# Gram products made one chunk per chunk, eight chunks ahead instead of ten

## Chip, cores and metric

The kernel runs on one core of a Trainium2 chip. The metric is the device time of one execution in microseconds (us); lower is better. Engines are named as the profile names them: PE (TensorE matmul), DVE (VectorE), ACT (ScalarE), POOL (GpSimd), SP (SyncE, which issues nearly all DMAs).

## What is computed

Three layers stand one behind the other: a delta-rule attention over 32 sequences (4 batches of 8 heads, 768 steps, head dimension 48), a mixer with two 768 x 768 token matrices, and a feed-forward layer with 1536 hidden columns. The change touches the first alone:

```python
k_n = k / (np.linalg.norm(k, axis=-1, keepdims=True) + 1e-06)
for t in range(S):
    y[:, :, t] = np.einsum('bhd,bhde->bhe', q[:, :, t], state)
    v_old = np.einsum('bhde,bhd->bhe', state, kt)
    state = state + bt[:, :, :, None] * np.einsum('bhd,bhe->bhde', kt, vt - v_old)
```

## The kernel before

**Chunks and sets.** The 768 steps are cut into NC = 24 chunks of 32. Inside a chunk the recurrence becomes a triangular system: its 32 x 32 matrix is made of the Gram products of the chunk's keys, and it is inverted once. Four chunks form a set (NS = 6 sets, 0 to 5); set s holds chunks 4s to 4s+3. `inverse_work(s)` inverts all matrices of a set at once on DVE, with part of the products on POOL, and ends in the transposed inverse `pt` (line 425). The chunk of index c needs the `pt` of set c // 4.

**The chunk loop** (lines 604 to 650) runs over c = 1 to 23. A chunk has two half steps, one for each half h of the sequences. In a half step PE computes `RW` from the state (line 437), DVE subtracts it from the values (`Rs`, line 440), PE multiplies by the inverse (line 452), ACT copies the product into `bdw` (line 458), PE adds to the state (`S`, line 466) and ACT copies the state into `bds` (line 471). PE takes the halves in turn: `S` of the half step before, then the product with `pt`, an output product, then `RW` of the next half step. In what follows, (h,c) is the half step h of chunk c, and the DVE rows `Rs`, two to a chunk, mark the time at which it begins.

**Gram products.** `a_work(c)` (line 162) computes for a later chunk the products of its keys with block diagonal tiles `bdk` (line 174): 16 matmuls; ACT copies them out into `G_sb` (keys with keys) and `mt` (keys with queries), and POOL masks `mt`. There are two `bdk` tiles, filled from DRAM by `spread(c + 2)` at the end of `a_work(c)` (line 155, two DMAs on the SP queue). So each tile is filled again only after the Gram products that read it.

**The order of DVE's inversion** is set by a planner. `Stream` (line 51) holds the items of all sets in a list of stages: A and B of a set, then C of that set together with A of the next (C is drawn first), then B of the next. Each item has an estimated cost. In each half step `dv.run(budget)` issues items for 3.08 us (2.3 us from chunk 14 on); what an item costs beyond the budget is kept as a debt in `due`, and the next half step starts with it. Some items are not `ready` before something else has been issued: the first item of A, `tg` (line 260, the transposition of `G_sb` into `Gi`), wants the Gram products of all four chunks of its set issued, that is `4 * s + 3 in done`. Where nothing is ready, `run` stops and the rest of the budget is lost.

**Forced ends.** At the end of a set, `pt` must exist for the next chunk, so the loop issues whatever is left, without a budget, before it goes on:

```python
        if (c % 4 == 3 and s + 1 < NS) or c == 18:
            while s + 1 not in PT:
                if not dv.step():
                    norms()
```

This debt stands in `due` as well. The last set is forced at c = 18, as the pools of the inversion are closed there (`mid.close()`), and the first weights of the mixer are loaded into memory that comes free then (lines 1156 to 1160).

Of the kernel before, what the change touches and what calls it, by code (L numbers as in the profile page):

```python
# [16 lines left out]
NC = 24  # L17
# [75 lines left out]
def attention(ctx, tc, kq, ktok, vin, betai, maskin, x, psa, late=None):  # L93
# [32 lines left out]
    def load_kq(c, part=slice(0, 2)):  # L126
        if c < NC:
            if c not in KQ:
                KQ[c] = ring(c).tile([128, 2, 4, 4, 32], F32, name="kqt")
            nc.sync.dma_start(out=KQ[c][:, part], in_=kq[c][:, part])  # L130

    def load_kt(c):
        if c < NC:
            KT[c] = ktp.tile([128, 4, 2, D], F32, name="ktt")
            nc.sync.dma_start(out=KT[c], in_=ktok[c])

    def load_v(c):
        if c < NC:
            V[c] = vp.tile([128, 8, D], F32, name="vt")
            nc.sync.dma_start(out=V[c], in_=vin[c])  # L140

    def scale_v(c):
        if c < NC:
            k = c % 4
            nc.gpsimd.tensor_tensor(out=V[c], in0=V[c], in1=bc(NT[c // 4][:, 8 * k:8 * k + 8].unsqueeze(2), [128, 8, D]),
                                    op=ALU.mult)
# [3 lines left out]
    def spread(c):  # L150
        if c >= NC:
            return
        for e in range(2):
            ee = slice(64 * e, 64 * e + D)
            nc.sync.dma_start(out=bdk[c % 2][ee, e], in_=kq[c, ee].rearrange("p k g r i -> p k (g r) i"))
# [6 lines left out]
    def a_work(wk, c):  # L162
        hold = {}
        dense = c >= 4

        def first():
            MT[c] = ring(c).tile([128, 4, 2, 32], F32, name="mt")
            hold[0] = psa.tile([128, 4, 2, 64], F32, name="pa", tag="pa")
            if not dense:
                hold[1] = psy.tile([128, 4, 2, 64], F32, name="py")  # L170

        def mm(g):
            for r in range(4):
                nc.tensor.matmul(hold[0][32 * r:32 * r + 32, g, :, :].rearrange("p e (k i) -> p e k i", k=2),  # L174
                                 KQ[c][:, 0, g, r, :], bdk[c % 2][:, :, :, 4 * g + r, :], start=True, stop=True)

        def mm1(g, e):
            for r in range(4):
                nc.tensor.matmul(hold[e][32 * r:32 * r + 32, g, e, 32:64], KQ[c][64 * e:64 * e + D, 0, g, r, :],
                                 KQ[c][64 * e:64 * e + D, 1, g, r, :], start=True, stop=True)  # L180

        def ev(src, e0, ne):
            if ne == 2:
                t = src.rearrange("p g e i -> p (g e) i")
                nc.scalar.copy(out=G_sb[c // 4 % 2][:, 8 * (c % 4):8 * (c % 4) + 8, :], in_=t[:, :, 0:32])
                nc.scalar.copy(out=MT[c].rearrange("p g e i -> p (g e) i"), in_=t[:, :, 32:64])
            else:
                nc.scalar.copy(out=MT[c][:, :, e0, :], in_=src[:, :, e0, 32:64])

        def fin():  # L190
            masks.append(c)
            if step[0] >= 0:
                cut()
            if dense:
                done.add(c)
                spread(c + 2)

        wk.add(0.0, first)
        if dense:
            for g in range(4):  # L200
                wk.add(0.29, lambda g=g: mm(g))
            wk.add(0.0, lambda: ev(hold[0], 0, 2))
        else:
            for g in range(4):
                for e in range(2):
                    wk.add(0.19, lambda g=g, e=e: mm1(g, e))
            for e in range(2):
                wk.add(0.0, lambda e=e: ev(hold[e], e, 1))
        wk.add(0.0, fin)
# [3 lines left out]
    def cut():  # L213
        while masks:
            t = MT[masks.pop(0)].rearrange("p g e i -> p (g e) i")
            nc.gpsimd.tensor_tensor(out=t, in0=t, in1=bc(mask, [128, 8, 32]), op=ALU.mult)
# [226 lines left out]
    def W(h, c, Rs):  # L443
        W_mm(h, c, Rs)
        W_out(h, c)
# [43 lines left out]
    def ym_work(wk, c):  # L489
        def m(e):  # L490
            for g in range(4):
                nc.tensor.matmul(Y[c][32 * g:32 * g + 32, e, :, :], MT[c][:, g, e, :],  # L492
                                 bdw[g // 2][c % NB][:, 2 * (g % 2) + e, :, :], start=(c == 0 and e == 0),
                                 stop=(e == 1),                                 skip_group_check=True)

        def ev():
            ys = p2.tile([128, 2 * 4 * D], F32, name="ys")
            nc.scalar.copy(out=ys, in_=Y[c].rearrange("p e r d -> p (e r d)"))
            o = 32 * (c % 4)
            for g in range(4):  # L500
                nc.sync.dma_start(out=x[c // 4][o:o + 32, g, :], in_=ys[32 * g:32 * g + 32, :])

        for e in range(2):
            wk.add(0.4, lambda e=e: m(e))
        wk.add(0.0, ev)
# [27 lines left out]
    def norms():  # L533
        for s in sorted(norm):
            if ("tg", s) in done:
                norm.pop(s)()
        while pend:
            pend.pop(0)()
# [65 lines left out]
    for c in range(1, NC):  # L604
        s = c // 4
        step[0] = c
        load_kq(c + 11)
        load_v(c + 5)
        scale_v(c + 2)
        load_kt(c + 2)  # L610
        wa, wm, wq = Work(), Work(), Work()
        for n in {1: (9, 10), 2: (11, 12)}.get(c, (c + 10,)):
            if n < NC:
                a_work(wa, n)
        ym_work(wm, c - 1)
        yq_work(wq, c)
        R0 = R(0, c)
        budget = 2.3 if c >= 14 else 3.08
        if c % 4 == 1 and c > 1 and s + 1 < NS:
            while ("tg", s + 1) not in done:  # L620
                dv.step()
        dv.run(budget)
        if late:
            late(c, 0)
        wa.run((0.0 if c == 2 else 0.42) * wa.left())
        S(1, c - 1)
        W(0, c, R0)
        norms()
        wm.flush()
        R1 = R(1, c)  # L630
        dv.run(budget)
        if late:
            late(c, 1)
# [4 lines that stand above are left out]
        wa.flush()  # L638
        S(0, c)
        W(1, c, R1)  # L640
        norms()
        wq.flush()
        if c == 13:
            soon.close()
        if c == 18:
            mid.close()
        if c == 19:
            early.close()
        if late:
            late(c, 2)  # L650
# [474 lines left out]
def build(tc, a):  # L1125
# [8 lines left out]
    with tc.manual_schedule(), outer:  # L1134
# [12 lines left out]
        wts = Weights(nc, None, wide)  # L1147

        def late(c, k):
            if (c, k) == (13, 2):  # L1150
                xp2 = ph1.enter_context(tc.tile_pool(name="x_", bufs=1, **R))
                x.extend(xp2.tile([128, 4, C], F32, name=f"x{t}") for t in (4, 5))
            if (c, k) == (18, 2):
                nc.gpsimd.memset(ones.bitcast(F32), 1.0)
                nc.scalar.copy(out=ones, in_=ones.bitcast(F32))
                wts.st = ph1.enter_context(tc.tile_pool(name="st", bufs=1, **R))
                mx.load_theta(ph1, tc, a["wth"], wts)
                wts.load()
                nc.sync.dma_start(out=ident, in_=a["ident"])
                nc.sync.dma_start(out=g, in_=a["g"])  # L1160
            if (c, k) == (19, 2):
                mx.open(ph1, tc)
                for s in range(3):
                    mx.load_w(s, a["wtok"], mx.cst if s < 2 else None, wts)
                wts.load()
            if c > 19 or (c, k) == (19, 1):
                wts.step()
            if (c, k) == (16, 2):
                nc.scalar.activation(out=warm, in_=warm, func=AF.Sin)
            if (c, k) == (20, 2):  # L1170
                mx.trans(0)
            if (c, k) == (21, 2):
                mx.theta(0)
                mx.angles(0)
                mx.trans(1)
            if (c, k) == (22, 1):
                mx.sines()
            if (c, k) == (22, 2):
                mx.cosines()
            if (c, k) == (22, 2):  # L1180
                mx.turn(0)
                mx.rest(0)
            if (c, k) == (23, 0):
                mx.theta(1)
                mx.angles(1)
            if (c, k) == (23, 1):
                mx.sines()
            if (c, k) == (23, 2):
                mx.cosines()
# [42 lines left out]
        n = len(MIX)  # L1232
# [115 lines left out]
```

## Time and profile before

| | |
|---|---|
| time, median of 3 runs | 786.51 us (785.75 to 788.28) |
| the profiled execution's own time | 786.73 us |
| its span, first to last instruction | 784.8 us |
| busy share of the span: PE, DVE, ACT, POOL | 90%, 66%, 45%, 27% |
| mean granted clock of PE | 0.969 |

The profile is of one execution. Times inside it are counted from the start of its span; its own time is 1.9 us longer than the span. The chunk loop lies at about 43 to 230 us, the mixer follows to about 425 us, then the feed-forward layer. PE's share is a mean over these stages and says nothing of the chunk loop by itself.

### The profile page before, as it was taken

What the parts mean: (1) busy time and instruction counts of PE and PEld (TensorE: products, weight loads), DVE (VectorE), ACT (ScalarE), POOL (GpSimd) and SP (SyncE); (2) the same over time, 40 slices, a digit from 0 to 9 for tenths busy, and PEclk for the clock granted to TensorE, in tenths of its full rate; (3) what the DMA queues carried; (4) which work ended last, traced back from release to release, by engine and by line L of the source; (5) the groups of instructions that cost most, each with busy time, mean ns of one, the idle gap of its engine ahead of it and who ended that gap; (6) DMA issues with size and microseconds to landing.
All of it is one profiled execution on the core that took longest, in us unless ns stands there. A gap on an engine that the chain in (4) does not pass through costs nothing.

```text
span 784.8 us, 18939 instructions
## 1 busy us (share of the span) xinstructions
PE 709.4 (90%) x7955; PEld 655.4 (84%) x7956; DVE 517.8 (66%) x875; ACT 356.9 (45%) x785; POOL 213.2 (27%) x234
## 2 busy tenths in 40 slices
PE   4577887777778999999997999999999999999997
PEld 3455555554468999999997999999999999999997
DVE  7987989986877888888876755435353534444342
ACT  2276776786775766654444433131322222131211
POOL 5854755744020001211111433113131221121120
PEclk8699999999989999999999999999999999999999
DMA  8975767234444223532432220000000000000000
GB/s 250 248 225 172 201 189 214 83 86 137 153 152 162 88 75 101 165 118 80 121 101 81 101 81 5 26 1 31 1 31 1 31 1 30 1 9 24 1 31 30
DMA packets 29716, 71.39 MB, mean 91 GB/s; under 512 B 4928, under 2 KB 17472, under 8 KB 29632
## 3 DMA queue, kind: packets, MB, share of 16 engines
q1 hardware_dynamic: 29632, 70.19, 29.0%
q8 instruction: 62, 1.02, 0.6%
q14 instruction: 22, 0.18, 0.1%
HBM read 56.02 MB, written 9.44 MB: 83 GB/s over the span
## 4 chain that ended last, share of the span: by engine, by line
PE 64%; DVE 15%; DMA 6%; ACT 6%; issue 5%; POOL 2%; SPq 1%; ACTq 0%; DVEq 0%; POOLq 0%
PE ph L1071 19%; PE acc L1090 19%; PE y L957 11%; PE pc L1012 5%; PE pth L897 3%; DMA bdk<-kq 3%; DVE prod L369 2%; ACT bdw L458 2%; DMA raw<-wtok 2%; PE py L492 1%; PE S L466 1%; PE pa L174 1%; DVE t L797 1%; PE RW L452 1%; DVE Ti L378 1%
## 5 line engine op out<-in xcount | busy, mean ns | idle before, releaser
L957 PE MATMUL y<-w,zh 128*128 128x384 f32 x576 | 154.8, 342 | 3.4 <-DVE u L966 2.4
L1090 PE MATMUL acc<-hh,f 128*128 128x384 f32 x576 | 147.0, 336 | 0.0
L1076 DVE SCALAR_TENSOR_TENSOR hl<-ph,hh 128x384 fp32r<-128x384 f32 x96 | 52.4, 553 | 114.5 <-ACT hh L1075 114.5
L1075 ACT ACTIVATE hh<-ph 128x384 fp32r<-128x384 f32 x96 | 46.7, 491 | 163.0 <-PE ph L1071 163.0
L1071 PE MATMUL ph<-xh,f 128*128 128x384 f32 x576 | 116.4, 337 | 0.4 <-DVE u L966 0.4
L957 PEld LDWEIGHTS y<-w,zh 128*128 128x128 f32 x576 | 105.8, 190 | 4.2 <-issue 2.7
L1090 PEld LDWEIGHTS acc<-hh,f 128*128 128x128 f32 x576 | 104.5, 188 | 0.0
L1071 PEld LDWEIGHTS ph<-xh,f 128*128 128x128 f32 x576 | 101.9, 188 | 0.7 <-issue 0.7
L957 PE MATMUL y<-w,zl 128*128 128x384 f32 x288 | 97.7, 339 | 2.4 <-DVE zl L938 2.4
L1090 PE MATMUL acc<-hl,f 128*128 128x384 f32 x288 | 96.9, 336 | 0.0
L1071 PE MATMUL ph<-xl,f 128*128 128x384 f32 x288 | 65.7, 336 | 0.0
L458 ACT COPY bdw<-RW 32x192 f32<-32x192 f32 x192 | 59.5, 310 | 13.6 <-PE RW L452 11.0
L957 PEld LDWEIGHTS y<-w,zl 128*128 128x128 f32 x288 | 54.6, 190 | 3.0 <-DVE zl L938 3.0
L471 ACT COPY bds<-S 48x384 f32<-48x384 f32 x92 | 43.5, 472 | 29.0 <-PE S L466 27.4
L466 PE MATMUL S<-bdw,ktt 128*48 128x192 f32 x368 | 42.0, 351 | 14.4 <-ACT bdw L458 14.3
L1090 PEld LDWEIGHTS acc<-hl,f 128*128 128x128 f32 x288 | 54.0, 188 | 0.0
L806 POOL TENSOR_TENSOR t<-t,g 128x384 f32<-128x384 f32 x12 | 15.3, 1279 | 135.3 <-DVE t L798 123.3
L1071 PEld LDWEIGHTS ph<-xl,f 128*128 128x128 f32 x288 | 51.6, 188 | 0.0
L452 PEld LDWEIGHTS RW<-Rs,pt 32*32 32x32 f32 x1472 | 19.8, 109 | 36.6 <-DVE Rs L440 28.5
L452 PE MATMUL RW<-Rs,pt 32*32 32x48 f32 x1472 | 26.4, 210 | 21.4 <-DVE Rs L440 21.0
L466 PEld LDWEIGHTS S<-bdw,ktt 128*48 128x48 f32 x368 | 20.8, 128 | 28.7 <-ACT bdw L458 22.2
L1100 POOL TENSOR_TENSOR o<-u,o 128x384 f32<-128x384 f32 x21 | 20.8, 1017 | 85.0 <-DVE o L1099 85.0
(165 smaller groups left out, 1305.8 us busy)
## 6 DMA issues: line engine op xcount, KB each, us to landing
kqt<-kq SPq DMA_DIRECT2D x20, 512.0 KB, 5.5
raw<-wtok SPq DMA_DIRECT2D x12, 768.0 KB, 4.7
raw<-wff SPq DMA_DIRECT2D x12, 768.0 KB, 4.9
bdk<-kq SPq DMA_DIRECT2D x40, 192.0 KB, 4.0
vt<-vin SPq DMA_DIRECT2D x24, 192.0 KB, 4.9
ktt<-ktok SPq DMA_DIRECT2D x24, 192.0 KB, 4.6
x<-ys SPq DMA_DIRECT2D x96, 48.0 KB, 2.5
flat<-t SPq DMA_DIRECT2D x12, 384.0 KB, 5.5
```

The source lines that it names most:

```text
L452: nc.tensor.matmul(RW[h][rr, 1, j, :], PT[c // 4][rr, m0 + j, :], Rs[rr, j, :], start=True, stop=True)
L458: nc.scalar.copy(out=b[rr, :, r, :], in_=RW[h][rr, 1, :, :])
L466: nc.tensor.matmul(S_ps[h][64 * e:64 * e + D, g, :], KT[c][:, 2 * h + g, e, :], b[:, 2 * g + e, :, :], start=(c == 0 and g == 0), stop=Tru ...
L471: nc.scalar.copy(out=n[ee, :, e, :], in_=S_ps[h][ee, :, :].rearrange("p g (r d) -> p (g r) d", r=4))
L897: nc.tensor.matmul(ps, l[:, k], self.tw[w][:, k], start=(n == 0), stop=(n == 8))
L957: nc.tensor.matmul(self.Y[q], l[:, ri, 128 * k:128 * k + 128], self.W[s][w][:, 2 * ri + h], start=(first and w == ri == 0 and l is zh), st ...
L1012: nc.tensor.matmul(ps, self.wc[w][:, k, 128 * e:128 * e + 128], r[:, k], start=(n == 0), stop=(n == 8))
L1071: nc.tensor.matmul(ps, w[:, 0, 128 * k:128 * k + 128], r[:, k], start=(n == 0), stop=(n == 8))
L1075: nc.scalar.activation(out=hh, in_=ps, func=AF.Relu)
L1076: nc.vector.scalar_tensor_tensor(out=hl, in0=ps, scalar=0.0, in1=hh.bitcast(F32), op0=ALU.max, op1=ALU.subtract)
L1090: nc.tensor.matmul(self.ACC[j][e], w[:, 1, 128 * e:128 * e + 128], r, start=(f == 0 and n == 0), stop=(f == NF - 1 and n == 2))
L1100: (nc.vector if j == NJ - 1 else nc.gpsimd).tensor_tensor(out=o, in0=u[:, e], in1=o, op=ALU.subtract)
```

## The change

Before, chunk 1 makes the Gram products of chunks 9 and 10, chunk 2 those of 11 and 12, and every later chunk c those of c + 10. Now every chunk c makes those of c + 8. The last one (chunk 23) is thus made in chunk 15 instead of 13, so the pool of the `bdk` tiles (`soon`) is closed at c = 15, and the tiles x4 and x5, which take its memory, are made there too.

```diff
         wa, wm, wq = Work(), Work(), Work()
-        for n in {1: (9, 10), 2: (11, 12)}.get(c, (c + 10,)):
-            if n < NC:
-                a_work(wa, n)
+        if c + 8 < NC:
+            a_work(wa, c + 8)
         ym_work(wm, c - 1)
...
         wq.flush()
-        if c == 13:
+        if c == 15:
             soon.close()
...
         def late(c, k):
-            if (c, k) == (13, 2):
+            if (c, k) == (15, 2):
                 xp2 = ph1.enter_context(tc.tile_pool(name="x_", bufs=1, **R))
```

Since the first item of a set waits for its four Gram products, the planner puts DVE's work in another order. Three places show it, all on DVE. In the rows, `Rs` is the subtraction that starts a half step, `Gi<-G` is `tg`, `XT` and `Ti` are the inversion's products and sums, `s`, `rc`, `nb`, `N` belong to the norms at the start of A, `prod` (DVE) and `prodp` (POOL) are its product tiles.

First, the end of set 1, in chunk 3. Before, between half step (0,3) and (0,4):

```order
L378 TENSOR_REDUCE XT<-prodp 128x16x4
L260 STREAM_TRANSPOSE Gi<-G_133 128x1024
L369 TENSOR_TENSOR prod<-R,XT 128x1024
L369 TENSOR_TENSOR prod<-R,XT 128x768
L440 TENSOR_TENSOR Rs_1223<-vt,RW_127 128x192
L279 TENSOR_SCALAR s_1225<-s_1199 128x32
L378 TENSOR_REDUCE Ti_132<-prod 128x4x16
L283 RECIPROCAL rc<-s_1225 128x32
L378 TENSOR_REDUCE Ti_132<-prod 128x4x16
L284 TENSOR_SCALAR sh<-s_1225 128x32
L425 STREAM_TRANSPOSE pt<-Ti_132 128x32x32
L440 TENSOR_TENSOR Rs_1309<-vt,RW_126 128x192
```

And now, from the same sum of XT on, as far as (1,4):

```order
L378 TENSOR_REDUCE XT<-prodp 128x16x4
L369 TENSOR_TENSOR prod<-R,XT 128x1024
L369 TENSOR_TENSOR prod<-R,XT 128x768
L378 TENSOR_REDUCE Ti_132<-prod 128x4x16
L440 TENSOR_TENSOR Rs_1175<-vt,RW_127 128x192
L378 TENSOR_REDUCE Ti_132<-prod 128x4x16
L425 STREAM_TRANSPOSE pt<-Ti_132 128x32x32
L440 TENSOR_TENSOR Rs_1251<-vt,RW_126 128x192
L260 STREAM_TRANSPOSE Gi<-G_133 128x1024
L440 TENSOR_TENSOR Rs_1314<-vt,RW_127 128x192
```

The transposition of set 2 and its first norms have moved from between the last steps of set 1 to behind its `pt`. The same happens at the ends of sets 2, 3 and 4.

Second, chunk 16. Before, from (0,16) to (0,17), set 5 stands at the end of A and in B:

```order
L440 TENSOR_TENSOR Rs_3143<-vt,RW_126 128x192
L312 TENSOR_TENSOR prod<-N_200,Ti_132 128x196
L313 TENSOR_REDUCE Ti_132<-prod 128x4x7
L369 TENSOR_TENSOR prod<-Gi,Ti_132 128x256 x2
L378 TENSOR_REDUCE XT<-prod 128x2x8x4
L440 TENSOR_TENSOR Rs_3204<-vt,RW_127 128x192
L378 TENSOR_REDUCE XT<-prodp 128x2x8x4
L369 TENSOR_TENSOR prod<-R,XT 128x256 x2
L378 TENSOR_REDUCE Ti_132<-prod 128x2x4x8
L440 TENSOR_TENSOR Rs_3271<-vt,RW_126 128x192
```

Now, from the `pt` of set 4 to the first norm behind (0,17):

```order
L425 STREAM_TRANSPOSE pt<-Ti_131 128x32x32
L440 TENSOR_TENSOR Rs_3105<-vt,RW_126 128x192
L440 TENSOR_TENSOR Rs_3155<-vt,RW_127 128x192
L260 STREAM_TRANSPOSE Gi<-G_134 128x1024
L440 TENSOR_TENSOR Rs_3217<-vt,RW_126 128x192
L279 TENSOR_SCALAR s_3219<-s_3184 128x32
```

Between (0,16) and (1,16) nothing of the inversion stands any more, and set 5 only begins behind (1,16).

Third, the end of set 5 in chunk 18. Before, from (0,18) to (0,19):

```order
L440 TENSOR_TENSOR Rs_3392<-vt,RW_126 128x192
L378 TENSOR_REDUCE XT<-prodp 128x16x4
L369 TENSOR_TENSOR prod<-R,XT 128x1024
L369 TENSOR_TENSOR prod<-R,XT 128x768
L440 TENSOR_TENSOR Rs_3456<-vt,RW_127 128x192
L378 TENSOR_REDUCE Ti_132<-prod 128x4x16 x2
L425 STREAM_TRANSPOSE pt<-Ti_132 128x32x32
L440 TENSOR_TENSOR Rs_3536<-vt,RW_126 128x192
```

Now the last twelve of the sixteen rows from (1,18) to (0,19); `Rs` of (1,18) stands four rows ahead of the first:

```order
L369 TENSOR_TENSOR prod<-R,XT 128x256 x2
L378 TENSOR_REDUCE Ti_132<-prod 128x2x4x8
L378 TENSOR_REDUCE Ti_132<-prodp 128x2x4x8
L369 TENSOR_TENSOR prod<-Gi,Ti_132 128x1024
L369 TENSOR_TENSOR prod<-Gi,Ti_132 128x768
L378 TENSOR_REDUCE XT<-prod 128x16x4 x2
L378 TENSOR_REDUCE XT<-prodp 128x16x4 x2
L369 TENSOR_TENSOR prod<-R,XT 128x1024
L369 TENSOR_TENSOR prod<-R,XT 128x768
L378 TENSOR_REDUCE Ti_132<-prod 128x4x16 x2
L425 STREAM_TRANSPOSE pt<-Ti_132 128x32x32
L440 TENSOR_TENSOR Rs_3536<-vt,RW_126 128x192
```

Before, three rows of the inversion stood in the last half step of chunk 18; now all of B and C of set 5 does, in one piece with no `Rs` inside it. From (0,19) on, DVE's rows are the same as before.

## Rows read from the trace of the kernel before

**Rows 1.** Busy time by stretch: span part, length, engines (count), PE clock, DMA.

```profile
72.20:163.43 91.23, 73.87 (x2216) 51.79 (x2216) 83.09 (x172) 66.09 (x184) 52.76 (x65) 0.94 0.60 170
163.43:185.95 22.52, 16.12 (x488) 10.60 (x488) 19.41 (x28) 18.52 (x48) 13.28 (x16) 1.00 0.31 86
...
425.00:784.00 359.00, 353.63 (x2019) 352.75 (x2019) 162.51 (x277) 97.19 (x186) 71.37 (x67) 1.00 0.08 28
```

**Rows 2.** What DVE waited for from 72.2 to 163.5: total, times, longest.

```profile
DVE Ti L309 <- POOL N L303: 2.1, 4, 0.5
DVE Rs L440 <- PE RW L437: 1.9, 4, 0.5
DVE prod L369 <- ACT R L327: 1.8, 3, 0.7
```

**Rows 3.** Timeline, DVE: start, length, row, [idle before]; (0,2), XT, (0,3), (1,3), (0,4), (0,16), (0,19).

```profile
50.29 0.35 DVE L440 TENSOR_TENSOR Rs<-vt,RW 128x192 f32<-128x192 f32 x1 [1.34 <-PE RW L437]
...
57.67 0.67 DVE L378 TENSOR_REDUCE XT<-prodp 128x64 f32<-128x512 f32 x1
61.74 0.35 DVE L440 TENSOR_TENSOR Rs<-vt,RW 128x192 f32<-128x192 f32 x1 [3.40 <-PE RW L437]
...
67.44 0.35 DVE L440 TENSOR_TENSOR Rs<-vt,RW 128x192 f32<-128x192 f32 x1 [0.70 <-PE RW L437]
...
72.20 0.36 DVE L440 TENSOR_TENSOR Rs<-vt,RW 128x192 f32<-128x192 f32 x1
...
163.43 0.35 DVE L440 TENSOR_TENSOR Rs<-vt,RW 128x192 f32<-128x192 f32 x1 [0.51 <-PE RW L437]
...
185.95 0.31 DVE L440 TENSOR_TENSOR Rs<-vt,RW 128x192 f32<-128x192 f32 x1
```

**Rows 4.** Timeline, PE, in chunks 2 and 3.

```profile
60.95 0.27 PE L481 MATMUL py<-bds,kqt 128*32 128x96 f32 x2 [1.68 <-issue]
...
62.73 0.65 PE L174 MATMUL pa<-bdk,kqt 128*32 128x128 f32 x16 [1.09 <-DMA bdk<-kq]
```

**Rows 5.** Timeline, DVE, the end of set 1 (first row) and of set 5.

```profile
64.27 2.47 DVE L369 TENSOR_TENSOR prod<-R,XT 128x1024 f32<-128x1024 f32 x2
...
177.41 0.41 DVE L378 TENSOR_REDUCE XT<-prodp 128x64 f32<-128x256 f32 x1
177.93 3.19 DVE L369 TENSOR_TENSOR prod<-R,XT 128x1024 f32<-128x1024 f32 x2
...
184.04 2.01 DVE L425 STREAM_TRANSPOSE pt<-Ti 128x1024 f32<-128x1024 f32 x1 [0.66 <-POOL Ti L385]
```

**Rows 6.** Timeline, DVE, transpositions of sets 2 and 5, set 4's last sum and pt.

```profile
62.34 2.01 DVE L260 STREAM_TRANSPOSE Gi<-G 128x1024 f32<-128x1024 f32 x1
...
151.26 1.99 DVE L260 STREAM_TRANSPOSE Gi<-G 128x1024 f32<-128x1024 f32 x1
153.16 0.92 DVE L378 TENSOR_REDUCE Ti<-prod 128x64 f32<-128x768 f32 x1
...
155.08 2.12 DVE L425 STREAM_TRANSPOSE pt<-Ti 128x1024 f32<-128x1024 f32 x1
```

**Rows 7.** Timeline, PE, two half steps of chunks 16 and 17.

```profile
164.06 0.86 PE L466 MATMUL S<-bdw,ktt 128*48 128x192 f32 x8 [0.76 <-ACT bdw L458]
...
167.34 0.86 PE L466 MATMUL S<-bdw,ktt 128*48 128x192 f32 x8 [0.76 <-ACT bdw L458]
```

**Rows 8.** Timeline, DVE, where B of set 5 begins.

```profile
164.48 0.98 DVE L369 TENSOR_TENSOR prod<-Gi,Ti 128x256 f32<-128x256 f32 x2
```

**Rows 9.** Timeline, SP's queue, the mixer's first weights.

```profile
186.08 0.33 SPq L717 DMA_DIRECT2D raw<-wth  x1
```

**Rows 10.** Busy time by stretch: the half step behind pt of sets 1, 2, 3.

```profile
72.20:75.00 2.80, 2.39 (x84) 1.93 (x86) 2.15 (x12) 2.32 (x8) 0.63 (x1) 1.00 0.94 230
103.00:106.30 3.30, 2.85 (x81) 2.24 (x81) 2.99 (x13) 1.71 (x5) 0.89 (x2) 0.73 0.94 270
130.90:134.20 3.30, 2.90 (x92) 2.83 (x96) 2.99 (x13) 1.24 (x4) 0.84 (x2) 0.64 0.46 120
```

## The prediction

> **What bounds the kernel now.** I read the busy time by stretch first. From 425 us on PE is busy 353.63 of 359.00 us, so that part only shifts. In the chunk loop, from half step (0,4) to (0,16), DVE is busy 83.09 of 91.23 us, PE 73.87 and ACT 66.09 [rows 1]. The table of waits says why DVE isn't busy there: 2.1 us for POOL, 1.9 for PE and 1.8 for ACT, 5.8 together [rows 2]. The loop is thus paced by DVE, which has a fixed list of work (the inversions) to do before set 5's pt. The question is how much DVE idles on the way to that pt. As marks I take the starts of three half steps on DVE: (0,4) at 72.20, (0,16) at 163.43 and (0,19), the first row behind set 5's pt, at 185.95 [rows 3]. The DVE rows before (0,2) stand in the same order before and after; behind (0,19) too.
>
> **1. Up to (0,4): the double load goes.** Before (0,3) DVE is done at 58.34 (57.67 + 0.67) and waits 3.40 us for PE, and 0.70 more at (1,3) [rows 3]. PE in turn stands still in chunks 2 and 3: 1.68 us in the output products and 1.09 for a bdk transfer [rows 4]. Chunk 2 issued two sets of Gram products; with one set in chunks 1 and 2 each, no bdk tile is wanted right behind its refill. I let both waits fall to 0, and the 1.34 us at (0,2) by half, 0.7 (ends 0 and 1.34). (0,3) then comes at 57.7.
>
> From there set 1 ends without set 2's rows in between, so the last sum of XT lies 0.6 us behind (0,3), at 58.3. What then ends last is POOL: at the end of set 5, where nothing was woven in before either, pt begins 6.2 us behind the end of that sum (177.41 + 0.41 to 184.04), and it waits 0.66 us for POOL's share [rows 5]. So pt begins at 64.5, and 1.9 us later (184.04 to 185.95) comes (0,4), at 66.4: **5.8 us earlier** than now.
>
> **2. From (0,4) to (0,16).** DVE's work here is now 91.23 - 5.8 = 85.4 us. Added are the transposition of set 2 (1.9 us, 62.34 to 64.27) and three of its norm rows (0.6, an estimate from the time that is left up to (0,4)), which stood before (0,4). Taken out is what set 5 had done by (0,16): from 151.26 to 163.43 are 12.2 us; less two waits of 0.5, three Rs of 0.3, set 4's last sum (0.8) and its pt (2.0) [rows 6], 7.5 remain. That makes 85.4 + 2.5 - 7.5 = 80.4.
>
> One price is new. Where the transposition stood between XT and the two products prod<-R, these took 2.47 us; where they follow XT directly, and so run beside POOL's first product on the same tiles, 3.19 [rows 5]. Sets 2 and 3 change from the one to the other (set 4 ended in the direct order already): 1.4 us. Work is then 81.8.
>
> The waits, for each of the three sets 2, 3, 4: for N on POOL 0.5 (2.1 by four), for R on ACT 0.6 (1.8 by three), for pt on POOL 0.7. For PE it was 0.5 a time. Now there is less to fill the half steps behind pt: the first has only the transposition, 1.9 us and 0.3 for Rs, while a half step that PE and ACT pace takes 3.28 us (164.06 to 167.34, with PE waiting 0.76 for ACT in each) [rows 7]. That could idle 1.1 us in the first and about as much in the next two, yet debts of time from longer half steps close part of it. I take 1.5 us a set, between 0.5 (as now) and 3.0. Chunk 15, with its budget of 2.3 us, gets 1.0 besides (3.28 - 2.3). Together 3 x 3.3 + 1.0 = 10.9, and the stretch is 81.8 + 10.9 = **92.7 us** against 91.2. (0,16) falls at 159.1, still 4.3 us early.
>
> **3. From (0,16) to (0,19): here the lead is missed.** Set 4's forced end leaves a debt, so the first half step of chunk 16 gets no DVE work at all, the second only the transposition, and the two of chunk 17 and the first of 18 some 2 us of small rows each. None fills 3.28 us, so these five half steps go at the pace of PE and ACT: 16.4 us. Then all of B and C of set 5 stands between (1,18) and (0,19). Its work I take from now: of 22.52 us DVE is busy 19.41 [rows 1]; less six Rs of 0.3 and the two rows ahead of B (0.8, as B begins at 164.48) [rows 8], 16.9. With one Rs (0.3) and pt's wait on POOL (0.9, as the Rs that now hides part of it moves away) the piece takes 18.1. The stretch is 34.5 us against 22.5: **12.0 longer**.
>
> **Behind (0,19)** nothing covers it: the mixer's first weights are issued at 186.08, right as set 5's pt (184.04 + 2.01) has ended, since they go into its memory [rows 9]. So what (0,19) loses the end loses. The later closing of the bdk pool costs nothing: x4 is first written in chunk 17, when the last Gram products (chunk 15) are two chunks back. Chunks 14 and 15 get 16 matmuls of Gram products each, two ACT copies and one POOL mask; PE waits 0.76 us per half step there [rows 7], which hides the matmuls, and if the copies aren't hidden, that is within the 1.5 us above.
>
> **Sum:** -5.8 + 1.5 + 12.0 = +7.7 us. The profiled execution took 786.73 us, 0.2 above the median of the runs, so the forecast is 794.4 us.
>
> **Rivals.**
>
> *A colder PE.* Behind pt of sets 2 and 3 PE's granted clock is 0.73 and 0.64 over the next half step, so part of it went at 1.2 GHz; behind set 1's it is 1.00 (2.4 GHz), and 81 matmuls take 2.85 us of PE where 84 took 2.39 [rows 10]. Today DVE's own work covers that. With less to do behind each pt, it shows: some 0.5 us in each of two half steps, behind four ends of sets, 4 us: 798.4. For it speaks that PE will wait longer for each pt; against it that set 1's restart was not cold.
>
> The Trainium skill ("TensorE: Matmul & The Clock Gate", section "What's actually happening") says that a gate passes half the clock's pulses unless the array is kept busy. By that rule every restart here is cold and the time is this rival's 798.4, and not 794.4; the rows agree in two cases of three, which is why it gets a chance of its own, and not the forecast.
>
> *The half step has no floor (the other side).* If 3.28 us is itself only what DVE leaves to PE and ACT, then the half steps shrink to DVE's rows. PE's waits (3 x 1.5 + 1.0) and those for R (1.8) vanish, and the five half steps of part 3 take 1.9 us each, 9.5 in place of 16.4: 14.2 us less than forecast, 780.2, faster than now. It decides from an average of about 2.1 us in those five on, if the waits vanish too. Against it: PE waits for bdw, not for Rs, in a row of half steps of equal length [rows 7].
>
> *The late pt is partly absorbed.* Behind 186 us the mixer's preparation also waits for transfers. If half of the 7.7 us fell into such waits, 790.6; if nearly all, about 787.5. Against it stands that the first of these transfers itself waits for pt [rows 9].
>
> **How the numbers follow.** The forecast, with its own spread of 790 to 799, gets 0.70; the colder PE 0.15 (797 to 802); absorption 0.10 (of it 0.05 within 2.4 us of now); no floor 0.05 (0.04 faster). Under 0.3% (2.4 us) a measurement of this kernel can hardly tell from no change. That gives faster 0.04, same 0.06, slower 0.90. The unknown costs give as bounds: at the low end PE's waits of part 2 at 0.5 a set (-3.0), the wait at (0,2) gone (-0.7) and the half steps of part 3 at 3.0 (-1.4), 789.3; at the high end 3.0 a set (+4.5) and the full wait at (0,2) (+0.7), 799.6. The range is 789.5 to 799.5; it leaves out no floor, most of the absorption and the upper part of the colder PE.
>
> **What would show it.** Right, if (0,4) comes near 66.4, (0,16) near 159 and (0,19) near 194 us, if the wait of 3.40 us at (0,3) is gone, if DVE does nothing of the inversion between (0,16) and (1,16), if sixteen rows in one piece of some 18 us end at set 5's pt with PE waiting, and if the mixer's first weights are issued right behind it. Part 1 is wrong if PE still stands still in chunk 2; part 2, if waits for PE between (0,4) and (0,16) sum to under 2 or over 10 us; part 3, if chunks 16 and 17 take well under 6.5 us each. The whole forecast is wrong if (0,19) comes no later than 188.

## The result, and the profile after

| | before | after |
|---|---|---|
| time, median of 4 runs each | 787.39 us (785.75 to 788.46) | 794.92 us (794.5 to 796.29) |
| the profiled execution's own time | 786.73 us | 794.5 us |
| its span | 784.8 us | 792.7 us |
| mean granted clock of PE | 0.969 | 0.955 |

The change makes the kernel slower: the ratio to before is 1.0115, with an interval of 1.0087 to 1.0142 (the two medians alone give 1.0096). Forecast were 794.4 us and slower.

The page's head of the kernel after, with busy time, share of the span and instructions of each engine:

```profile
span 792.7 us, 18925 instructions
...
PE 714.0 (90%) x7956; PEld 660.2 (83%) x7956; DVE 521.9 (66%) x875; ACT 355.9 (45%) x785; POOL 210.9 (27%) x234
```

The shares of busy time are those of before. An average over the span hides what happened; the stretches show it. Busy time by stretch of the kernel after, columns as in [rows 1]; the marks are again the starts of (0,4), (0,16) and (0,19):

```profile
66.44:158.40 91.96, 75.57 (x2312) 53.11 (x2304) 81.56 (x154) 68.71 (x191) 52.68 (x67) 0.96 0.62 179
158.40:193.10 34.70, 17.27 (x480) 11.25 (x480) 26.01 (x50) 17.46 (x45) 12.26 (x17) 0.80 0.15 42
434.00:792.00 358.00, 353.83 (x2022) 352.89 (x2020) 162.50 (x277) 96.21 (x185) 71.45 (x67) 1.00 0.08 27
```

(0,4) comes 5.8 us earlier (66.44 against 72.20), the next stretch takes 0.7 more (91.96 against 91.23), and the third 34.70 against 22.52: DVE idles 8.7 us in it (34.70 - 26.01), where it idled 3.1 (22.52 - 19.41), and does 6.6 us more work there. From (0,19) to the end of the span 599.6 us pass, before 598.85. The feed-forward layer has only moved.

DVE's timeline of the kernel after, at the end of set 1 and from (0,16) to (0,19), answers to [rows 3], [rows 5] and [rows 8]:

```profile
57.40 0.34 DVE L440 TENSOR_TENSOR Rs<-vt,RW 128x192 f32<-128x192 f32 x1
57.66 0.41 DVE L378 TENSOR_REDUCE XT<-prodp 128x64 f32<-128x256 f32 x1
58.17 3.74 DVE L369 TENSOR_TENSOR prod<-R,XT 128x1024 f32<-128x1024 f32 x2
...
64.28 2.13 DVE L425 STREAM_TRANSPOSE pt<-Ti 128x1024 f32<-128x1024 f32 x1
66.44 0.35 DVE L440 TENSOR_TENSOR Rs<-vt,RW 128x192 f32<-128x192 f32 x1
...
158.40 0.34 DVE L440 TENSOR_TENSOR Rs<-vt,RW 128x192 f32<-128x192 f32 x1
161.87 0.35 DVE L440 TENSOR_TENSOR Rs<-vt,RW 128x192 f32<-128x192 f32 x1 [3.13 <-PE RW L437]
162.15 1.98 DVE L260 STREAM_TRANSPOSE Gi<-G 128x1024 f32<-128x1024 f32 x1
164.45 0.35 DVE L440 TENSOR_TENSOR Rs<-vt,RW 128x192 f32<-128x192 f32 x1 [0.33 <-PE RW L437]
168.47 0.35 DVE L440 TENSOR_TENSOR Rs<-vt,RW 128x192 f32<-128x192 f32 x1 [1.25 <-PE RW L437]
171.83 0.35 DVE L440 TENSOR_TENSOR Rs<-vt,RW 128x192 f32<-128x192 f32 x1 [0.66 <-PE RW L437]
175.11 0.35 DVE L440 TENSOR_TENSOR Rs<-vt,RW 128x192 f32<-128x192 f32 x1 [0.98 <-PE RW L437]
175.38 0.75 DVE L369 TENSOR_TENSOR prod<-Gi,Ti 128x256 f32<-128x256 f32 x2
...
191.22 2.04 DVE L425 STREAM_TRANSPOSE pt<-Ti 128x1024 f32<-128x1024 f32 x1 [0.92 <-POOL Ti L385]
193.10 0.36 DVE L440 TENSOR_TENSOR Rs<-vt,RW 128x192 f32<-128x192 f32 x1
```

The wait of 3.40 us at (0,3) is gone. At (1,16) DVE has waited 3.13 us with nothing to do, and it waits for PE at every half step from there to (1,18). Then the rest of set 5 stands in one piece, from 175.11 to 193.10, with no half step in it. What it costs PE and what hangs on it stand on PE and on SP's queue:

```profile
193.52 0.86 PE L452 MATMUL RW<-Rs,pt 32*32 32x48 f32 x32 [9.88 <-DVE Rs L440]
```

```profile
193.32 0.33 SPq L716 DMA_DIRECT2D raw<-wth  x1
```

PE waits 9.88 us for (0,19), and the mixer's first weights are issued 0.06 us behind the end of pt (191.22 + 2.04), as in [rows 9]. What DVE waited for in the middle stretch (66.4 to 158.4) answers to [rows 2]:

```profile
DVE Rs L440 <- PE RW L437: 3.6, 4, 1.1
DVE s L279 <- ACT s L271: 1.6, 3, 0.5
DVE Ti L309 <- POOL N L303: 1.6, 3, 0.5
DVE prod L369 <- ACT R L327: 1.0, 3, 0.5
```

### The profile page after: what moved, and what is told of

Read it like the earlier page. It is cut to its first block, busy times and chain, and to the rows that moved or that the text cites. A ratio compares the mean times of both kernels' runs of the same rounds, so it can differ in the third digit from the quotient of the medians.

```text
span 792.7 us, 18925 instructions
## 1 busy us (share of the span) xinstructions
PE 714.0 (90%) x7956; PEld 660.2 (83%) x7956; DVE 521.9 (66%) x875; ACT 355.9 (45%) x785; POOL 210.9 (27%) x234
## 4 chain that ended last, share of the span: by engine, by line
PE 65%; DVE 18%; ACT 7%; issue 5%; POOL 3%; DMA 2%; ACTq 0%; SPq 0%; DVEq 0%; POOLq 0%
PE ph L1070 19%; PE acc L1089 19%; PE y L956 11%; PE pc L1011 5%; PE pth L896 3%; DVE prod L369 3%; ACT bdw L458 3%; DMA raw<-wtok 2%; DVE XT L378 2%; PE S L466 2%; DVE t L796 1%; PE RW L452 1%; PE py L481 1%; ACT bds L471 1%; POOL prodp L369 1%
```

## The experiments

The theory was the prediction's: the double loads cost time in chunk 2, and the lead that they buy is worth more at the end of set 5, where half steps run without DVE work and the work comes later in one piece. The rivals: the memory given back later costs something itself; the colder PE is the price; the double load would be cheap elsewhere. All times below are medians; the ratio is to runs of the kernel before on the same chip, whose medians were 786.84, 785.45 and 785.18 us in the three groups (787.39 beside the change itself), so kernels of different groups are compared by their ratios. The marks are those of each kernel's profiled execution, whose own time can lie some 2 to 3 us from the median (789.28 in e1, 795.25 in e2, 788.25 in e3). "Rest" is the span less the start of (0,19).

| kernel | (0,4) | (0,16) | (0,19) | rest | time, us | ratio (95%) |
|---|---|---|---|---|---|---|
| before | 72.20 | 163.43 | 185.95 | 598.9 | | 1 |
| after | 66.44 | 158.40 | 193.10 | 599.6 | 794.92 | 1.0115 (1.0087 to 1.0142) |
| e1_mem_late | 74.40 | 165.70 | 188.26 | 599.0 | 786.85 | 1.0000 (0.9979 to 1.0020) |
| e2_tail_late | 73.14 | 163.00 | 194.75 | 598.8 | 798.17 | 1.0138 (1.0110 to 1.0166) |
| e3_budget_full | 65.82 | 158.00 | 187.84 | 598.7 | 790.29 | 1.0046 (1.0029 to 1.0063) |
| e9_no_debt | 66.61 | 158.51 | 189.78 | 601.0 | 791.75 | 1.0074 (1.0053 to 1.0094) |
| e4_double_later | 66.71 | 160.54 | 188.07 | 599.1 | 790.36 | 1.0056 (1.0038 to 1.0074) |
| e7_ys_before | 71.29 | 160.76 | 183.28 | 597.7 | 782.28 | 0.9955 (0.9931 to 0.9978) |
| e8_ys_double | 68.10 | 154.22 | 181.78 | 599.7 | 785.35 | 0.9996 (0.9976 to 1.0016) |
| e5_lead9 | 69.93 | 157.53 | 183.82 | 599.9 | 783.93 | 0.9988 (0.9965 to 1.0011) |
| e6_lead9_budget | 69.41 | 159.68 | 182.50 | 598.6 | 782.96 | 0.9962 (0.9938 to 0.9985) |
| e10_ys_lead9_budget | 69.24 | 159.05 | 181.83 | 597.2 | 781.72 | 0.9948 (0.9927 to 0.9968) |
| e11_ys_double_budget | 67.90 | 159.85 | 182.29 | 599.1 | 782.77 | 0.9960 (0.9942 to 0.9979) |

One reading runs through all of them: (0,19) lies anywhere from 181.8 to 194.8 us, and the rest stays between 597.2 and 601.0. What (0,19) loses, the end loses.

**e1, the memory alone** (on the kernel before):

```diff
-        if c == 13:
+        if c == 15:
             soon.close()
-            if (c, k) == (13, 2):
+            if (c, k) == (15, 2):
```

> The kernel before, with only the second half of the change: the bdk pool is closed at chunk 15, and x4 and x5 are made there; the Gram products keep their lead of 10. Theory (the loss is DVE left without work by the late Gram products): no row of an engine moves, so no difference, ratio to the kernel before 0.998 to 1.002, (0,19) at 186 us. Rival (the later release of memory delays a transfer): slower by 3 to 8 us.

The ratio is 1.0000. The later giving back of the memory costs nothing that can be measured. (0,19) came at 188.26, where 186 was expected: this execution was already 2.2 us late at (0,4), in chunks that the edit doesn't touch (from 48 to 75 us PE waited 3.9 us for `bdk`, before 2.9).

**e2, the lead alone** (on e1): chunks 1 and 2 keep their double loads; from chunk 12 on the lead is 8, as chunks 10 and 11 make none.

```diff
-        for n in {1: (9, 10), 2: (11, 12)}.get(c, (c + 10,)):
+        for n in {1: (9, 10), 2: (11, 12), 10: (), 11: ()}.get(c, (c + 10 if c < 10 else c + 8,)):
```

> The kernel before as far as chunk 9, doubles in chunks 1 and 2 included; then chunks 10 and 11 make no Gram products and chunks 12 to 15 make those of 20 to 23, so only set 5 comes as late as in the change. Theory: the stall in chunks 2 and 3 is as before ((0,4) at 72 us), the end of set 5 goes as in the change, 34 to 35 us from (0,16) to (0,19) in place of 22.5; (0,16) comes no earlier than 162, since chunks 14 and 15 run at the pace of PE and ACT; (0,19) at 196 to 198, 796 to 799 us, slower than the change itself. Rival (what costs is the lead of 8 throughout, a colder PE behind each pt): not more than 4 us over the kernel before, 791.

Measured 798.17 us, 1.4% slower. The missing lead at the end alone costs 11 us, more than the whole change, which gains at the start what this kernel doesn't. (0,19) came at 194.75 and (0,16) to (0,19) took 31.75 us, both outside what was expected. The profiled execution was a short one (795.25 us; the median lies in the expected 796 to 799). And part of the loss lies ahead of (0,16), where DVE waited 1.86, 2.53 and 2.96 us in the last three half steps, and the transposition stood already in the first half step of chunk 16.

**e3, the change with the full budget in chunks 14 on:**

```diff
-        budget = 2.3 if c >= 14 else 3.08
+        budget = 3.08
```

> The change with one edit: the budget of 3.08 us per half step stays to the end in place of 2.3 from chunk 14 on. Gram products stand where the change has them, in chunks 14 and 15 too. Theory (what costs is DVE's empty half steps in chunks 15 to 18 and the piece that is left for chunk 18): set 4's forced end gets shorter, the transposition of set 5 comes into the first half step of chunk 16, the piece before set 5's pt shrinks, (0,19) comes 4 to 6 us earlier than in the change, 789 to 791 us. Rival (the Gram products of chunks 14 and 15, or the colder PE, cost the time): within 1.5 us of the change, 793.5 to 796.

Measured 790.29 us. Its busy time by stretch:

```profile
158.00:187.84 29.84, 16.04 (x488) 10.47 (x486) 26.01 (x49) 18.48 (x47) 13.09 (x17) 0.90 0.18 49
```

DVE does the same 26.01 us of work from (0,16) to (0,19) as after, in 29.84 us instead of 34.70. What this run wins back over the change is thus idle time of DVE in chunks 16 to 18: with a larger share drawn in each half step, 4.9 us of it vanish. Not all of the change's loss is idle time, though, as the part on the prediction shows.

**e9, the change with the debt struck out** behind each forced end:

```diff
                 if not dv.step():
                     norms()
+            dv.due = 0.0
```

> The change with one edit: the debt that a forced end leaves is struck out, so the half step behind each pt gets its full budget; the budget stays 2.3 from chunk 14 on. Theory: the transposition of set 5 moves up into the first half step of chunk 16, where DVE waits 3.13 us in the change, every later row of set 5 one half step earlier, the piece before set 5's pt is shorter by the work of one half step, some 2 us: (0,19) at 191 us, 792 to 793.5 us. Rival (the debt isn't what leaves that half step empty, or the work only changes places): as the change, 794.5 to 795.5.

Measured 791.75 us, with (0,19) at 189.78, both a little earlier than expected. The transposition moved into the first half step of chunk 16, and (0,16) to (0,19) is 3.4 us shorter than after:

```profile
158.51:189.78 31.27, 16.76 (x480) 11.07 (x480) 25.46 (x51) 17.55 (x45) 12.44 (x17) 0.83 0.16 46
```

So the debt of set 4's forced end, which leaves the first half steps of chunk 16 without work, is one cause of the idle time, and the small budget (e3) another. That rests on the trace: by the times alone e9 can't be told from the change, as their intervals overlap (1.0053 to 1.0094 against 1.0087 to 1.0142).

**e4, the double loads in chunks 6 and 10 instead of 1 and 2** (on the kernel before):

```diff
-        for n in {1: (9, 10), 2: (11, 12)}.get(c, (c + 10,)):
+        n0 = c + 8 + (c > 6) + (c > 10)
+        for n in (n0, n0 + 1)[:2 if c in (6, 10) else 1]:
```

> One Gram product set per chunk at the start as in the change (lead 8), but chunks 6 and 10 make two, so that from chunk 10 on the lead is 10 again and set 5 comes as early as before; bdk pool closed at 13 as before. Theory: the gain of part 1 stays ((0,4) at 66 to 67 us) and the loss of part 3 is gone ((0,16) to (0,19) 22 to 27 us): (0,19) at 184 to 187, 784 to 788 us. Rival (the double load costs wherever it stands, a wait for bdk): a stall of 3 us or more in chunks 6 and 10, over 790 us.

Here my theory failed, and the rival (a stall of 3 us or more where the double stands) came true: 790.36 us, where 784 to 788 was expected. (0,4) came early, at 66.71 as after, but from (0,4) to (0,8) passed 35.6 us (to 102.33), where after takes 30.5 (to 96.97). PE's timeline in chunks 6 and 7 and behind the double of chunk 10 (last row), and SP's queue in chunks 6 and 7, say why:

```profile
84.05 1.35 PE L174 MATMUL pa<-bdk,kqt 128*32 128x128 f32 x32 [1.62 <-DMA bdk<-kq]
...
92.23 1.08 PE L174 MATMUL pa<-bdk,kqt 128*32 128x128 f32 x16 [4.44 <-DMA bdk<-kq]
...
121.37 1.93 PE L174 MATMUL pa<-bdk,kqt 128*32 128x128 f32 x32 [3.22 <-DMA bdk<-kq]
```

```profile
84.32 3.48 SPq L501 DMA_DIRECT2D x<-ys  x4
87.90 1.92 SPq L155 DMA_DIRECT2D bdk<-kq  x4
```

The refill of the tiles stands on SP behind the four DMAs that write a chunk's outputs (`x<-ys`), which take SP 3.48 us. PE, and all behind it, waits 4.44 us for a transfer that SP had not yet issued.

**e7, that queue alone** (on the kernel before): up to chunk 11 the output DMAs are put into a list and issued behind the refills.

```diff
-            for g in range(4):
-                nc.sync.dma_start(out=x[c // 4][o:o + 32, g, :], in_=ys[32 * g:32 * g + 32, :])
+            held.append(out)
+            if c >= 12:
+                held.pop(0)()
...
         wa.flush()
+        while held:
+            held.pop(0)()
```

> The kernel before (two Gram product sets in chunks 1 and 2), but the four DMAs that carry a chunk's output to x are issued at the end of the Gram products, behind the refills of bdk, not ahead of them, up to chunk 11. Theory (PE's stall in chunks 2 and 3 is a bdk refill that stands late on SP's queue): the refills are issued 2 to 3 us earlier, the waits for bdk in chunks 2 and 3 get shorter, (0,4) at 68 to 71 us in place of 72 to 74, 783 to 786 us. Rival (the stall is the load of PE and ACT by two sets in a chunk, or instruction fetch): no change within 1 us.

What PE waited for from 48 to 75 us, first before, then in e7:

```profile
PE pa L174 <- DMA bdk<-kq: 2.9, 3, 1.1
```

```profile
PE pa L174 <- DMA bdk<-kq: 1.6, 1, 1.6
```

Measured 782.28 us, 0.45% faster than before, a little below the 783 to 786 that I gave, with (0,4) at 71.29, just outside the 68 to 71. Order on SP's queue cost the kernel before some 3.5 us, but that isn't the price of the double load alone, nor all of it: by the marks only 0.9 us of the gain stand at (0,4), 1.8 more come between (0,4) and (0,16), and (0,4) still lies 4.9 us behind that of the change.

**e8, e4 with the same list:**

> The run with the doubles in chunks 6 and 10 (790.4 us), with the outputs issued behind the refills as in the run above. Theory: the wait of 4.4 us for bdk in chunk 7 shrinks to 1 to 2 us and (0,8) comes 3 us earlier; 785 to 788 us. Rival: as it was, 789 to 791 us.

The refill now goes first, and PE's wait for `bdk` in chunks 6 and 7 is gone:

```profile
82.88 2.40 SPq L155 DMA_DIRECT2D bdk<-kq  x4
85.38 3.13 SPq L504 DMA_DIRECT2D x<-ys  x4
```

Measured 785.35 us, 0.6% less than e4 by the ratios and no difference to before; from (0,4) to (0,8) pass 30.25 us. So the order on SP's queue was the cause of e4's miss.

**e5, a lead of 9**, one double load, in chunk 1 (on the kernel before, pool closed at 14):

```diff
-        for n in {1: (9, 10), 2: (11, 12)}.get(c, (c + 10,)):
+        for n in {1: (9, 10)}.get(c, (c + 9,)):
```

> Chunk 1 makes the Gram products of 9 and 10, every later chunk c those of c + 9; the bdk pool is closed at 14, as the last set is made there. One double load in place of two, and set 5 can begin one chunk later than before the change, one earlier than in it. Theory: one stall for bdk of 1 to 4 us is left in chunk 2, (0,4) at 67 to 70 us; the piece before set 5's pt is shorter than the change's 18 us, (0,19) at 185 to 188 us, 785 to 789 us. Rival (the lateness of set 5 costs in proportion to the chunks it comes later): halfway between both kernels, 790 to 792 us.

(0,19) came at 183.82, 1.2 us earlier than the earliest that I gave, and the time is 783.93 us, under the 785 to 789 that I gave; it can't be told from before. One chunk more of lead than the change has brings 1.3% (ratio 0.9988 against 1.0115), some 10 us, although (0,4) comes 3.5 us later (69.93 against 66.44):

```profile
157.53:183.82 26.29, 16.01 (x488) 10.61 (x488) 20.90 (x39) 18.58 (x47) 13.00 (x17) 0.97 0.25 74
```

DVE still has 20.90 us of work behind (0,16), against 26.01 after, and is busy in all but 5.4 us.

**e6, e10 and e11, put together.** e6 is e5 with the full budget, e10 is e6 with e7's list, e11 is e8 with the full budget.

> As the run with a lead of 9, and the budget of 3.08 us per half step to the end. Theory: less is left for the piece in chunk 18, (0,19) another 0 to 2 us earlier, 783 to 788 us. Rival: with a longer list per half step PE waits more in chunks 14 to 17, and the time stays within 1 us of the run with a lead of 9 or gets longer.

> Three edits together: lead of 9, budget of 3.08 us to the end, outputs issued behind the bdk refills up to chunk 11. Theory (the stall in chunk 2 and the empty half steps are separate costs): the wait of 2 us for bdk in chunk 2 goes, (0,4) at 67 to 68, (0,19) at 180.5 to 182, 780 to 782 us, faster than the kernel before and the change. Rival: the stall is already covered there, 782.5 to 784 as with the lead of 9 and the full budget.

> Doubles in chunks 6 and 10, outputs behind the refills, budget of 3.08 us to the end. Theory: the piece in chunk 18, 12.7 us there from (0,18) to (0,19), shortens by 1 to 3 us, (0,19) at 179 to 181, 780 to 784 us. Rival: 785 us, as with the smaller budget.

All three are faster than before; e6's 782.96 lies just under the 783 to 788 that I gave. e10 has the lowest median, 781.72 us (0.9948, 0.9927 to 0.9968), and beats both kernels, but the intervals of e6, e7, e10 and e11 overlap, so the order among these four is open. e10's (0,4) missed its 67 to 68 (69.24): no wait for a refill is left, but PE stood still twice for "issue", 1.6 and 1.0 us. In e11 (0,19) came at 182.29 instead of 179 to 181; (0,18) to (0,19) did shrink, from 12.7 us in e8 to 7.1. But in chunk 7, where e8 has no wait for a refill, PE waited here, although the refill was issued ahead of the outputs; the profile puts the wait down to an output DMA, and no run tells why:

```profile
90.58 1.11 PE L174 MATMUL pa<-bdk,kqt 128*32 128x128 f32 x16 [2.97 <-DMA x<-ys]
```

## Why the prediction was right

**What bounds the kernel.** Right. DVE is busy 81.56 of 91.96 us from (0,4) to (0,16), and the end follows set 5's pt in every kernel that ran.

**1. Up to (0,4).** Forecast 66.4, measured 66.44. (0,3) was put at 57.7 and came at 57.40, pt at 64.5 and came at 64.28. The waits of PE in chunk 2 [rows 4] are gone. e4 and e7 add what the rows of before couldn't tell: the wait for `bdk` hangs in part on the order of SP's queue (1.6 us up to 75 us in e7, before 2.9; e1 and e2, with the same chunks 1 to 3 as before, show 3.9 and 4.0). The inner make-up was off: from the end of XT's last sum to pt I put POOL's share at the end, with a wait of 0.66 us. It was 6.21 us in all, as expected, but the length was in the pair prod<-R (3.74 us), and no wait for POOL followed; that the total agrees is luck.

**2. From (0,4) to (0,16).** Forecast 92.7, measured 91.96. The two parts of the sum were mis-sized: DVE's four groups of waits sum to 7.8 us and not 10.9, which leaves 84.2 us for the rest, where I had 81.8. For pt on POOL I put 0.7 a set; there was none. For PE I put 1.5 a set and 1.0 in chunk 15; 3.6 came in all, still within the 2 to 10 that the text allowed; the 1.6 us for ACT's `s` weren't in my list. Against that the pairs of sets 2 and 3 cost 2.5 us more (3.74 each, before 2.57 and 2.42), where I had put 1.4, and that of set 4 took 0.5 less (2.62, before 3.16), where I had put no change. The rest of the 2.4 isn't traced. The errors cancel in part and leave 0.7 us, which is luck.

**3. From (0,16) to (0,19).** Forecast 34.5, measured 34.70: five half steps of 16.7 us (175.11 - 158.40; forecast 16.4) and a piece of 18.0 (forecast 18.1). DVE did nothing of the inversion between (0,16) and (1,16). The causes that I named each have a run: the debt (e9, 3.4 us of this stretch back), the budget (e3, 4.9 back), the missing lead (e2 loses 11 us by it alone; e5 regains the time by one chunk of it). The two parts taken back overlap, as in both runs the transposition stands in the first half step of chunk 16; they weren't run together.

**Work and idle time.** I put 1.4 us for longer pairs; over the whole way to (0,19) the traces show more. From the start of the span to (0,19), before, after and in e3, with DVE's busy time as the third engine:

```profile
0.00:185.95 185.95, 135.54 (x4043) 94.84 (x4044) 162.16 (x310) 118.04 (x329) 111.07 (x142) 0.91 0.64 180
...
0.00:193.10 193.10, 135.74 (x4044) 96.05 (x4044) 165.56 (x309) 117.23 (x329) 108.71 (x142) 0.88 0.60 174
...
0.00:187.84 187.84, 134.34 (x4044) 95.60 (x4044) 166.94 (x309) 117.14 (x329) 108.60 (x142) 0.89 0.63 179
```

The list of work is the same. Of the 7.15 us by which (0,19) comes later, 3.75 are more idle time of DVE (27.54 against 23.79) and 3.4 are longer rows. Nearly all of the latter stand in the products prod<-R up to (0,19), first before, then after:

```profile
L369 DVE TENSOR_TENSOR prod<-R,XT 128x256 f32<-128x256 f32 (+2 forms) x24 | 22.8, 990 | 2.8 <-ACT R L327 2.4
...
L369 DVE TENSOR_TENSOR prod<-R,XT 128x256 f32<-128x256 f32 (+2 forms) x24 | 26.0, 1123 | 2.4 <-ACT R L327 1.6
```

So nearly half of the delay at (0,19) stands not in an empty planner but in pairs that run longer in the new order. e3 bears it out: DVE idles less there than before (20.90 us), and (0,19) still comes 1.9 us later. No run took the longer pairs away by themselves, so how much of this would come back without them stays open.

**Behind (0,19).** Forecast no change, measured +0.7 us, which the rests in the table (597.2 to 601.0) can't tell from none. In these two executions (0,20) follows 7.28 us behind (0,19), where it was 6.34. PE waits 9.88 us after and 1.18 before, and its granted clock in these two half steps is, first before, then after:

```profile
185.95:189.30 3.35, 2.99 (x66) 2.10 (x68) 0.31 (x3) 1.97 (x6) 2.49 (x5) 0.58 0.57 205
189.30:192.29 2.99, 2.69 (x88) 1.82 (x86) 1.95 (x5) 1.79 (x5) 0.00 (x0) 0.90 0.59 182
...
193.10:196.60 3.50, 3.08 (x66) 2.19 (x68) 0.37 (x2) 1.72 (x5) 2.49 (x5) 0.50 0.64 200
196.60:200.38 3.78, 3.72 (x90) 2.60 (x90) 2.04 (x5) 2.19 (x6) 0.00 (x0) 0.62 0.62 167
```

So the clock was already near half before in the first of them; most of the difference lies in the second.

**Sum.** Forecast +7.7 us on the span, measured +7.9 (792.7 - 784.8) in the two profiled executions and +7.5 between the medians.

**The rivals.** *No floor* fell: the five half steps took 3.3 us each on average. *Absorption* fell: the rest didn't shrink. *Colder PE* was half right, and its place was wrong. Behind pt of sets 1, 2 and 3 I had looked for it; there the clock is 1.00, 0.98 and 0.97, but in the half step ahead of (0,4), (0,8) and (0,12) it is near half (0.51, 0.54 and 0.57). Busy time by stretch of the kernel after: ahead of and behind (0,4) and (0,8), then behind pt of set 4:

```profile
62.90:66.40 3.50, 3.04 (x88) 2.90 (x92) 3.40 (x4) 1.24 (x4) 2.41 (x5) 0.51 0.62 164
66.40:69.40 3.00, 3.00 (x100) 2.07 (x96) 2.25 (x3) 1.60 (x5) 0.00 (x0) 1.00 0.73 235
93.40:96.90 3.50, 3.01 (x88) 2.88 (x92) 3.40 (x4) 1.25 (x4) 2.44 (x5) 0.54 0.68 180
97.00:100.00 3.00, 3.00 (x100) 2.06 (x95) 2.21 (x2) 1.58 (x5) 0.00 (x0) 0.98 0.77 236
...
158.40:161.90 3.50, 3.10 (x66) 2.22 (x68) 0.37 (x3) 1.72 (x5) 0.28 (x1) 0.52 0.00 0
161.90:164.50 2.60, 2.41 (x88) 1.64 (x86) 2.27 (x3) 1.68 (x5) 0.00 (x0) 0.99 0.24 61
```

PE waits for Rs of (1,3), ahead of the first of these, and restarts at 1.2 GHz:

```profile
63.36 0.86 PE L452 MATMUL RW<-Rs,pt 32*32 32x48 f32 x32 [2.55 <-DVE Rs L440]
```

But DVE is busy for 3.40 of those 3.50 us, so next to nothing can be lost. Only behind sets 4 and 5 does the slow half step stand uncovered, and there I estimate its cost over before at 0.2 us (3.47 against 3.28) and at most 0.9 (7.28 - 6.34). The rule of the Trainium skill ("TensorE: Matmul & The Clock Gate", section "What's actually happening"), that the clock is halved unless activity releases it, agrees at all five ends of sets (0.50 to 0.57). What it costs depends on whether DVE has work beside it: by this estimate 1.1 us here, not the rival's 4.

## What to carry to other kernels

A lead at the start of a pipeline is a stock of work for its end: before cutting it, look at which half steps near the last deadline would run with an empty planner, since work that isn't ready in time comes back in one piece that nothing covers. A new order of one engine's work also changes what it runs beside: here pairs of rows that run longer beside POOL's product make up nearly half of the delay. When a budget or a debt limits how much may be issued per step, it should be let go where a deadline is near. And a stall on a transfer is first to be looked for in the queue that issues it: moving four outputs behind the refills gave 0.45%, without touching the work.

## What was not expected of the hardware

**Which engine starts first decides the price of a pair.** POOL's first product and DVE's pair prod<-R read the same tiles. In the kernel after, at the ends of sets 1 and 2 (and 3), POOL starts first:

```profile
58.15 1.29 POOL L369 TENSOR_TENSOR prodp<-R,XT 128x512 f32<-128x512 f32 x1 [1.88 <-DVE XT L378]
...
88.68 1.28 POOL L369 TENSOR_TENSOR prodp<-R,XT 128x512 f32<-128x512 f32 x1 [1.87 <-DVE XT L378]
```

In the kernel before, at the end of set 5, DVE starts first, at 177.93 [rows 5]:

```profile
177.97 2.33 POOL L369 TENSOR_TENSOR prodp<-R,XT 128x512 f32<-128x512 f32 x1 [3.90 <-DVE XT L378]
```

In after POOL begins 0.02 us ahead of DVE (58.15 against 58.17), keeps its 1.29 us, and DVE's pair takes 3.74: 1.27 more than the 2.47 of the pair that stood apart from it [rows 5], the length of POOL's product. Where DVE begins 0.04 us ahead, POOL's product takes 2.33 and DVE's pair 3.19. The Trainium skill ("SBUF — State Buffer", section "Who interferes with whom") says that a DVE instruction with two inputs in SBUF contends with one of GpSimd that reads SBUF, that the port pair they share is an exclusive lock, and that the order of issue decides which one is blocked. These rows agree with it (3.74 against 3.19 us); no run changed that order alone.

**Issuing costs SP time.** In the rows shown four output DMAs hold SP's queue for 3.48 us in e4 and 3.13 in e8, some 0.8 to 0.9 us each, four refills 1.92 and 2.40. In e4 that made PE wait 4.44 us.

**Left open.** PE's stalls for "issue" (1.68 us in the kernel before [rows 4], 1.6 and 1.0 in e10) come at other places from kernel to kernel; no run tells why. The wait for `bdk` in chunk 2 differs between executions: e1, which doesn't touch chunk 2, reached (0,4) 2.2 us later than before. Whether the change would cost less if DVE's pair started ahead of POOL's product wasn't tried, nor a third `bdk` tile, with which a refill could be issued earlier.
